# One level of Strassen for the first product of the MLP, in eight of nine token tiles

## The chip, the core and the metric

The kernel runs on one core of a Trainium2 chip. The core has a matrix engine (TensorE, "PE" in the profile, with its weight loads shown apart as "PEld"), a vector engine (VectorE, "DVE"), an activation engine (ScalarE, "ACT"), a general engine (GpSimd, "POOL") and a queue for transfers (SyncE, "SP"). [...] The metric is the device time of one execution, in microseconds (us).

## The reference

What is computed, cut to what matters:

```python
# q, k, v: [8 batches, 8 heads, 576, 64], s: [8, 8, 576]; attention with a bias of cumulated s
x = attention(q, k, v, s)                      # [8, 576, 512]
u = x + real(fft(fft(x, axis=1), axis=2))
un = (u - mean(u)) / sqrt(var(u) + 1e-6)       # over the 512 channels
out = u + maximum(un @ w_ch1, 0) @ w_ch2       # w_ch1 [512, 2048], w_ch2 [2048, 512]
```

The change is in the last line alone, the MLP, and mostly in its first product `un @ w_ch1`.

## The kernel before

The 8 x 576 = 4608 tokens run as eight batches through attention and the Fourier step, which write `u` to a buffer `uD` in DRAM (channels on partitions). Then the MLP runs over nine tiles of 512 tokens (`TOK`). Its data are held in two parts, a high part that the matrix engine takes in its short fp32 form (`F32R`) and a low part, the rest; each product is therefore three matmuls (high x high, low weights x high, high weights x low).

`mlp_tile(t0, n)` walks over 16 slices `f` of 128 hidden channels (`NF` = 16). For each it issues 12 matmuls of 128x512 (L182: three kinds times four blocks `j` of 128 channels) into one PSUM bank `h`, then the relu on ACT (`zh`, L186) and its low part on DVE (`zl`, L187), and, one slice later, 12 matmuls of 128x512 of the second product (L195 to L197) into four banks `acc0` to `acc3` that are held over the whole tile. The scale 1/std (`r`) is applied at the end of the tile, so that the first product runs on `u - mu`, split into `uch` and `ucl`.

`load_w(pool, f)` puts slice `f` of both weight matrices into SBUF for good: `wh[f]` and `wl[f]`, 1024 columns each, of which the first 512 belong to the first product and the rest to the second. The weights arrive as 64-bit numbers. `rounded` turns 256 columns of them into f32 with DVE (L82, L84, L86, L87), ACT (L83) and POOL (L88). For slices 0 to 5 (`NC` = 6) that was done earlier, during attention, and the f32 weights lie in a DRAM buffer `wD`; slices 6 to 15 are rounded while the first MLP tile runs. After that ACT casts the high part (L111) and DVE (first half) or POOL (second half) subtracts for the low part (L113).

`ln_tile` makes `uch`, `ucl`, `mu` and `r` of the next tile: it loads `u` (1 MB), sums over channels by matmuls with ones (L122), and uses DVE (L145, L147, L153, the reciprocal L158), ACT (L146, L148) and POOL. The first tile runs woven with the Fourier step of the last batch (lines L250 to L328, tiles `pzs`, `pzc`, `pyc`, `pys`) and with the rounding of the weights. The order on each engine is set by a scheduler from the order in which the generators are woven; nothing is written out by hand. At the end of a tile DVE multiplies `acc` by `r` (L203), POOL rebuilds `u` from `uch + ucl + mu` (L209, L210) and adds it (L211), and SP stores the result. In the last tile that sum is made ahead (L169) and added on DVE (L205).

## Time and profile before

| | us |
|---|---|
| timed runs, median (lowest to highest of 3) | 1440.1 (1437.15 to 1442.24) |
| profiled execution, its span | 1436.6 |
| attention, Fourier, up to the first MLP tile | 0 to about 587 |
| first MLP tile, woven with the last batch and the rounding of weights | 587 to 714.8 |
| tiles 1 to 8 | 714.8 to 1431.0 |
| last multiply, add and store | 1431.0 to 1436.6 |

One execution is profiled. "PE busy" counts overlapping pipelined matmuls, each of which is shown from issue to its modelled end, so the length of one row (about 0.39 us for 128x512) is not its cost in a stream: the distance from one start to the next is. Where the timeline folds several equal instructions into one row (x4), its start is that of the first. Tables by stage give, for each stretch of time, the busy time of each engine with the number of instructions in brackets, then the mean granted clock of the matrix engine (1.00 is full), the share of the transfer engines' time and GB/s.

### The profile page before, as it was taken

What the parts mean: (1) busy time and instruction counts of PE and PEld (TensorE: products, weight loads), DVE (VectorE), ACT (ScalarE), POOL (GpSimd) and SP (SyncE); (2) the same over time, 40 slices, a digit from 0 to 9 for tenths busy, and PEclk for the clock granted to TensorE, in tenths of its full rate; (3) what the DMA queues carried; (4) which work ended last, traced back from release to release, by engine and by line L of the source; (5) the groups of instructions that cost most, each with busy time, mean ns of one, the idle gap of its engine ahead of it and who ended that gap; (6) DMA issues with size and microseconds to landing.
All of it is one profiled execution on the core that took longest, in us unless ns stands there. A gap on an engine that the chain in (4) does not pass through costs nothing.

```text
span 1436.6 us, 17960 instructions
## 1 busy us (share of the span) xinstructions
PE 1333.6 (93%) x6190; PEld 1072.2 (75%) x6190; DVE 746.5 (52%) x1684; ACT 540.7 (38%) x1211; POOL 550.9 (38%) x540
## 2 busy tenths in 40 slices
PE   4888979898989897998899999999999999999998
...
DVE  6577676778676778799833232132321323212212
...
GB/s 208 128 185 146 152 145 168 148 159 181 156 144 164 163 121 162 173 122 119 93 23 30 30 30 8 22 30 30 30 8 22 30 30 30 8 22 0 30 0 30
DMA packets 78166, 124.98 MB, mean 87 GB/s; under 512 B 11256, under 2 KB 36185, under 8 KB 78075
## 3 DMA queue, kind: packets, MB, share of 16 engines
...
q8 instruction: 49, 0.80, 0.2%
...
## 4 chain that ended last, share of the span: by engine, by line
PE 50%; DVE 7%; POOL 2%; DMA 1%; issue 1%; ACT 1%; SPq 0%; DVEq 0%; POOLq 0%; ACTq 0%
PE h L182 25%; PE acc L195 8%; PE acc L197 8%; PE acc L196 8%; POOL we L88 1%; DVE we L82 1%; DVE wm L87 1%; DVE wl L113 1%; DVE wm L84 1%; DVE we L86 1%; DVE Df L259 0%; POOL wl L113 0%; DMA raw<-in_wP_dram 0%; ACT wh L111 0%; DVE ucl L147 0%
## 5 line engine op out<-in xcount | busy, mean ns | idle before, releaser
L187 DVE SCALAR_TENSOR_TENSOR zl<-h,zh 128x512 fp32r<-128x512 f32 x144 | 98.6, 686 | 402.1 <-ACT zh L186 402.1
L186 ACT ACTIVATE zh<-h 128x512 fp32r<-128x512 f32 x144 | 85.8, 596 | 524.8 <-PE h L182 524.8
L197 PE MATMUL acc<-zl,wh 128*128 128x512 f32 x576 | 226.6, 394 | 4.2 <-DVE zl L187 4.2
L195 PE MATMUL acc<-zh,wh 128*128 128x512 f32 x576 | 227.2, 394 | 0.4 <-ACT zh L186 0.4
L196 PE MATMUL acc<-zh,wl 128*128 128x512 f32 x576 | 226.3, 393 | 0.0
L520 PE MATMUL pavB<-P,va 128*128 128x320 f32 (+2 forms) x640 | 200.8, 403 | 7.4 <-ACT stage L524 6.7
L456 PE MATMUL pm<-KQ 128*128 128x256 f32 (+4 forms) x384 | 159.6, 434 | 38.7 <-DVE Mx L463 18.9
L492 ACT ACTIVATE P<-ps 128x320 f32<-128x320 f32 (+4 forms) x384 | 145.5, 391 | 114.8 <-PE ps L489 109.7
L488 PE MATMUL ps<-KQ 128*128 128x256 f32 (+3 forms) x384 | 155.0, 406 | 22.7 <-ACT P L492 15.8
L182 PE MATMUL h<-uch,wh 128*128 128x512 f32 x576 | 159.0, 396 | 8.3 <-ACT wh L111 8.3
L463 DVE CUSTOM_DVE_ANT_0 trash<-pm,amask 128x128 bf16<-128x128 f32 (+3 forms) x256 | 123.6, 483 | 76.4 <-PE pm L456 60.0
L182 PE MATMUL h<-uch,wl 128*128 128x512 f32 x576 | 159.0, 398 | 0.8 <-DVE wl L113 0.8
L182 PE MATMUL h<-ucl,wh 128*128 128x512 f32 x576 | 158.4, 396 | 0.0
L211 POOL TENSOR_TENSOR o<-o,w 128x512 f32<-128x512 f32 x32 | 42.1, 1316 | 249.6 <-issue 216.5
L182 PEld LDWEIGHTS h<-uch,wh 128*128 128x128 f32 x576 | 107.6, 189 | 35.7 <-ACT wh L111 12.0
L197 PEld LDWEIGHTS acc<-zl,wh 128*128 128x128 f32 x576 | 108.3, 188 | 30.8 <-DVE zl L187 5.8
L520 PEld LDWEIGHTS pavB<-P,va 128*128 128x128 f32 (+1 forms) x640 | 106.5, 197 | 31.1 <-issue 13.0
L182 PEld LDWEIGHTS h<-uch,wl 128*128 128x128 f32 x576 | 109.4, 190 | 26.7 <-DVE wl L113 1.5
L182 PEld LDWEIGHTS h<-ucl,wh 128*128 128x128 f32 x576 | 109.7, 190 | 25.0
L195 PEld LDWEIGHTS acc<-zh,wh 128*128 128x128 f32 x576 | 108.5, 188 | 25.3 <-ACT zh L186 0.8
L196 PEld LDWEIGHTS acc<-zh,wl 128*128 128x128 f32 x576 | 108.5, 188 | 24.8
L489 PE MATMUL ps<-q,k 128*128 128x256 f32 (+3 forms) x384 | 121.4, 319 | 0.0
(139 smaller groups left out, 2025.9 us busy)
## 6 DMA issues: line engine op xcount, KB each, us to landing
...
```

The lines of the kernel that those rows point to most:

```text
L182: nc.tensor.matmul(h[:, :n], a[:, j * 128:(j + 1) * 128], b[:, j, :n], start=i == 0, stop=i == 11)
L186: nc.scalar.activation(zh[:, :n], h[:, :n], AF.Relu)
L187: nc.vector.scalar_tensor_tensor(out=zl[:, :n], in0=h[:, :n], scalar=0.0, in1=zh[:, :n].bitcast(F32), op0=ALU.max, op1=ALU.subtract)
L195: nc.tensor.matmul(acc[j][:, :n], a[:, cs], y[:, :n], start=g == 0, stop=False)
L196: nc.tensor.matmul(acc[j][:, :n], b[:, cs], y[:, :n], start=False, stop=False)
L197: nc.tensor.matmul(acc[j][:, :n], a[:, cs], z[:, :n], start=False, stop=g == NF - 1)
L456: nc.tensor.matmul(p[:nq, :n], qy[:, h, 128 * c:128 * c + nq], ky[:, h, k0:k0 + n], start=True, stop=True)
L463: nc.vector.tensor_tensor_reduce(out=trash[:nq, :n], in0=p[:nq, :n], in1=amask[:nq, m0:m0 + n], scale=1.0, scalar=first if x else NEG, op0 ...
L488: nc.tensor.matmul(p[:nk, :n], ky[:, h, ksl], qy[:, h, a:a + n], start=True, stop=False)
L489: nc.tensor.matmul(p[:nk, :n], k1[:, h, ksl], q1[:, h, a:a + n], start=False, stop=True)
L492: nc.scalar.activation(P[:nk, o:o + a + n - lo], p[:nk, lo - a:n], AF.Exp, scale=0.125)
L520: nc.tensor.matmul(p[:, a - lo:n], va[:nk, c, vs], P[:nk, o:o + w], start=c == 0, stop=c == cs[-1])
```

## The change

The first product of tiles 1 to 8 is no longer computed slice by slice. Two hidden slices `f` = 2g and 2g+1 form a pair `g` (eight pairs). The 256 x 512 block of weights of the pair is seen as 2 x 2 blocks, and so is the tile's 512 channels x 512 tokens; one level of Strassen (Winograd's form) gives the four result blocks from seven products instead of eight. Each product is 6 matmuls of 128x256 (three kinds times two blocks of 128 channels; L338). Per pair there are 7 x 6 = 42 matmuls of 256 columns where there were 24 of 512. The four sums of weight blocks per pair are made once (`sums_w`: on POOL L144, DVE L153, L158, L161, L164, splits on ACT L148 and DVE L149) and kept in `sh[g]`, `sl[g]` (one sum overwrites `wh`, `wl`); the four sums of data blocks are made for each tile (`combine`, L230 to L233) and all seven blocks are split (`block`: ACT L221, DVE L222). The results are gathered out of PSUM by ACT copies (L342, L346, L348) and DVE adds (L344, L350, L353) before the relu (L330, L331).

The second halves of the weights no longer stay in SBUF. For slices 6 to 15 they are rounded as before and stored to `wD` (L120), and `load_w2(f)` loads 256 KB from there (L127), casts (ACT, L128) and subtracts (POOL, L129) for each slice of each of the nine tiles, into four buffers used in turn. `u` for the last addition is loaded again from `uD` rather than rebuilt (L275; in the last tile L268).

The first tile (`first_tile`) keeps the plain product, in two halves of 256 tokens (24 matmuls of 128x256 for each slice, L299). The second product is the same 12 matmuls of 128x512 (L249 to L251). In tiles 1 to 8 the order on the matrix engine is the order of the code: the pair before has 24 matmuls of the second product left, in 8 groups of 3, and after each of the seven block products stands one of these groups (after the last, two).

```diff
-            m = wl[:, xs].bitcast(F32) if f < NC else (yield from rounded(stage, f, x, nstage))
-            nc.scalar.copy(wh[:, xs], m)
...
-            (nc.vector if x * n < 512 else nc.gpsimd).tensor_sub(wl[:, xs], m, wh[:, xs].bitcast(F32))
...
-                for a, b in ((wh, uch), (wl, uch), (wh, ucl)):
-                    for j in range(4):
-                        nc.tensor.matmul(h[:, :n], a[:, j * 128:(j + 1) * 128], b[:, j, :n], start=i == 0, stop=i == 11)
...
+        wh = pool.tile([128, 512], F32R, tag=f"wh{f}", name=f"wh{f}")
+        wl = pool.tile([128, 512], F32R, tag=f"wl{f}", name=f"wl{f}")
         W[f] = (wh, wl)
         if f < NC:
+            nc.sync.dma_start(out=wl.bitcast(F32), in_=wD[f, :, 0:512])
+            nc.scalar.copy(wh, wl.bitcast(F32))
+            yield 0.2
+            nc.vector.tensor_sub(wl, wl.bitcast(F32), wh.bitcast(F32))
+            yield 0.2
+            return
+        for x in range(1024 // WC):
+            xs = slice(WC * x, WC * x + WC)
+            m = yield from rounded(stage, f, x, nstage)
+            if x < 2:
+                nc.scalar.copy(wh[:, xs], m)
+                yield 0.1
+                nc.vector.tensor_sub(wl[:, xs], m, wh[:, xs].bitcast(F32))
+            else:
+                nc.sync.dma_start(out=wD[f, :, xs], in_=m)
+            yield 0.1
...
+    def load_w2(f):
+        h = w2p.tile([128, 512], F32R, tag="w2h", name="w2h", bufs=4)
+        low = w2p.tile([128, 512], F32R, tag="w2l", name="w2l", bufs=4)
+        nc.sync.dma_start(out=low.bitcast(F32), in_=wD[f, :, 512:1024])
+        nc.scalar.copy(h, low.bitcast(F32))
+        nc.gpsimd.tensor_sub(low, low.bitcast(F32), h.bitcast(F32))
+        W2[f] = (h, low)
+    def sums_w(g):
+        (ah, al), (ch, cl) = W[2 * g], W[2 * g + 1]
+        sh = sp.tile([128, 768], F32R, tag=f"sh{g}", name=f"sh{g}")
+        sl = sp.tile([128, 768], F32R, tag=f"sl{g}", name=f"sl{g}")
+        def tmp():
+            return sx.tile([128, 256], F32, tag="sx", name="sx", bufs=5)
+        def whole(h, low, x):
+            t = tmp()
+            xs = slice(256 * x, 256 * x + 256)
+            nc.gpsimd.tensor_add(t, h[:, xs].bitcast(F32), low[:, xs].bitcast(F32))
+            return t
+        def parts(t, h, low):
+            nc.scalar.copy(h, t)
+            nc.vector.tensor_sub(low, t, h.bitcast(F32))
+        a21 = whole(ch, cl, 0)
+        a22 = whole(ch, cl, 1)
+        nc.vector.tensor_add(a22, a21, a22)
+        yield 1.0
+        parts(a22, ch[:, 0:256], cl[:, 0:256])
+        a11 = whole(ah, al, 0)
+        s2 = tmp()
+        nc.vector.tensor_sub(s2, a22, a11)
+        parts(s2, sh[:, 0:256], sl[:, 0:256])
+        yield 1.0
+        nc.vector.tensor_sub(a21, a11, a21)
+        parts(a21, sh[:, 256:512], sl[:, 256:512])
+        a12 = whole(ah, al, 1)
+        nc.vector.tensor_sub(a12, a12, s2)
+        parts(a12, sh[:, 512:768], sl[:, 512:768])
+        yield 1.0
+        SW[g] = (sh, sl)
...
+    def block(t0, k, src):
+        h = bp.tile([128, 2, 256], F32R, tag="bh", name="bh", bufs=9)
+        low = bp.tile([128, 2, 256], F32R, tag="bl", name="bl", bufs=9)
+        nc.scalar.copy(h, src)
+        nc.vector.tensor_sub(low, src, h.bitcast(F32))
+        BL.setdefault(t0, {})[k] = (h, low)
+    def combine(t0):
+        u, _ = LN[t0]
+        b11, b12, b21, b22 = (quarter(u, i, k) for i in range(2) for k in range(2))
+        t3, t2, t4 = (ltmp(x).rearrange("p (j t) -> p j t", j=2) for x in ("t3", "t2", "t4"))
+        nc.gpsimd.tensor_sub(t3, b22, b12)
+        nc.vector.tensor_sub(b12, b12, b11)
+        nc.vector.tensor_sub(t2, b22, b12)
+        nc.vector.tensor_sub(t4, b21, t2)
+        return [b11, b21, t2, b12, t3, b22, t4]
...
+        def issue(entry, j):
+            acc, y, z, f, done = entry
+            a, b = W2[f]
+            cs = slice(j * 128, (j + 1) * 128)
+            nc.tensor.matmul(acc[j], a[:, cs], y, start=f == 0, stop=False)
+            nc.tensor.matmul(acc[j], b[:, cs], y, start=False, stop=False)
+            nc.tensor.matmul(acc[j], a[:, cs], z, start=False, stop=f == NF - 1)
+            if f == NF - 1:
+                done(j)
...
+                w = op.tile([128, TOK], F32, tag="w", name="w", bufs=2)
+                nc.sync.dma_start(out=w, in_=uD[j, :, t0:t0 + TOK])
+            nc.vector.tensor_mul(o, r, acc[j])
+            (nc.vector if last else nc.gpsimd).tensor_add(o, o, w)
+            (nc.scalar if last and j % 2 else nc.sync).dma_start(out=out[j, :, t0:t0 + TOK], in_=o)
...
+            if f + 1 < NF:
+                load_w2(f + 1)
+            wh, wl = W[f]
+            h = bank("h")
+            for k in range(2):
+                i = 0
+                for a, b in ((wh, 0), (wl, 0), (wh, 1)):
+                    for j in range(4):
+                        nc.tensor.matmul(h[:, 256 * k:256 * k + 256], a[:, j * 128:(j + 1) * 128], bl[j // 2, k][b][:, j % 2], start=i == 0, stop=i == 11)
+                        i += 1
+            zh = zp.tile([128, TOK], F32R, tag="zh", name="zh", bufs=3)
+            zl = zp.tile([128, TOK], F32R, tag="zl", name="zl", bufs=3)
+            nc.scalar.activation(zh, h, AF.Relu)
+            nc.vector.scalar_tensor_tensor(out=zl, in0=h, scalar=0.0, in1=zh.bitcast(F32), op0=ALU.max, op1=ALU.subtract)
...
+    def fast_tile(t0, side):
+        _, r = LN[t0]
+        bl = BL.pop(t0)
+        acc = done = None
+        for g in range(NF // 2):
+            load_w2(2 * g)
+            load_w2(2 * g + 1)
+            todo = groups()
+            n = len(todo)
+            (ah, al), (ch, cl) = W[2 * g], W[2 * g + 1]
+            sh, sl = SW[g]
+            lo, hi = slice(0, 256), slice(256, 512)
+            A = [(ah[:, lo], al[:, lo]), (ah[:, hi], al[:, hi]), (sh[:, 0:256], sl[:, 0:256]), (ch[:, lo], cl[:, lo]),
+                 (sh[:, 256:512], sl[:, 256:512]), (sh[:, 512:768], sl[:, 512:768]), (ch[:, hi], cl[:, hi])]
+            b1 = hx.tile([128, 512], F32, tag="hx", name="b1") if g % 2 == 0 else bank("b1")
+            b2, b3 = bank("b2"), bank("b3")
+            cs = cp.tile([128, 3, 256], F32, tag="cs", name="cs", bufs=2)
+            z = [[zp.tile([128, TOK], F32R, tag=t, name=t, bufs=3) for t in ("zh", "zl")] for _ in range(2)]
+            def relu(y, at, src):
+                nc.scalar.activation(y[0][:, at], src, AF.Relu)
+                nc.vector.scalar_tensor_tensor(out=y[1][:, at], in0=src, scalar=0.0, in1=y[0][:, at].bitcast(F32), op0=ALU.max, op1=ALU.subtract)
+            for k, (p, start) in enumerate(((b1, True), (b2, True), (b1, False), (b3, True), (b1, False), (b3, False), (b1, False))):
+                bh, low = bl[k]
                 i = 0
+                for a, b in ((A[k][0], bh), (A[k][1], bh), (A[k][0], low)):
+                    for j in range(2):
+                        nc.tensor.matmul(p[:, 0:256], a[:, j * 128:(j + 1) * 128], b[:, j], start=start and i == 0, stop=i == 5, skip_group_check=not start)
                         i += 1
+                p = p[:, 0:256]
+                if k == 0:
+                    nc.scalar.copy(cs[:, 0], p)
+                elif k == 1:
+                    nc.vector.tensor_add(cs[:, 0], cs[:, 0], p)
+                elif k == 2:
+                    nc.scalar.copy(cs[:, 1], p)
+                elif k == 3:
+                    nc.scalar.copy(cs[:, 2], p)
+                elif k == 4:
+                    nc.vector.tensor_add(cs[:, 2], cs[:, 2], p)
+                    relu(z[1], hi, cs[:, 2])
+                elif k == 5:
+                    nc.vector.tensor_add(cs[:, 1], cs[:, 1], p)
+                    relu(z[0], slice(0, 512), cs[:, 0:2].rearrange("p a t -> p (a t)"))
+                else:
+                    relu(z[1], lo, p)
+                for x in range(n * k // 7, n * (k + 1) // 7):
+                    todo[x]()
+                side(g, k)
+            if g == 0:
+                acc = accs()
+                done = writer(t0, acc, r)
+            held.extend((acc, z[x][0], z[x][1], 2 * g + x, done) for x in range(2))
...
+    def early(t0):
+        blocks.extend(combine(t0))
+        for k in range(5):
+            block(t0, k, blocks[k])
+            yield 1.0
+    blocks = []
+    weave([first_tile(tiles[0]), NF], [chain(idle(1000), mixing), FOURIER * 0.6], [ahead(), 100],
+          [later(chain(ln_tile(tiles[1], 1), early(tiles[1])), 4), 16])
+    for _ in feed:
+        pass
+    for k in range(5, 7):
+        block(tiles[1], k, blocks[k])
+    for g in range(2):
+        weave([sums_w(g), 1.0])
...
+            if x == 1 and k % 2 == 0 and g + 2 < NF // 2:
+                if k == 0:
+                    adding[0] = sums_w(g + 2)
+                next(adding[0], None)
```

The matrix engine inside a tile, before: `h` is the bank of the first product, `acc` those of the second; after three rows of four L182, one for each kind, stand groups of three L195, L196, L197 (three of the four groups are shown).

```order
2998 L182 MATMUL h<-uch,wh_7463 128x512 x4
2999 L182 MATMUL h<-uch,wl_7464 128x512 x4
3000 L182 MATMUL h<-ucl,wh_7463 128x512 x4
3001 L195 MATMUL acc_8317<-zh,wh_7384 128x512 [waits Activation_49]
3002 L196 MATMUL acc_8317<-zh,wl_7385 128x512
3003 L197 MATMUL acc_8317<-zl,wh_7384 128x512 [waits DVE_49]
3004 L195 MATMUL acc_8318<-zh,wh_7384 128x512
3005 L196 MATMUL acc_8318<-zh,wl_7385 128x512
3006 L197 MATMUL acc_8318<-zl,wh_7384 128x512
3007 L195 MATMUL acc_8319<-zh,wh_7384 128x512
3008 L196 MATMUL acc_8319<-zh,wl_7385 128x512
```

The matrix engine in the first pairs of a later tile, after: `b` are the banks of the block products, `bh` and `bl` the split data blocks, `sh` and `sl` the split weight sums, `w2h` and `w2l` the second weights.

```order
2684 L338 MATMUL b_8344<-bh,sh_8088 128x256 [waits Activation_49]
2685 L338 MATMUL b_8344<-bh,sh_8088 128x256
2686 L338 MATMUL b_8344<-bh,sl_8089 128x256 x2
2687 L338 MATMUL b_8344<-bl,sh_8088 128x256 x2
2688 L249 MATMUL acc_8196<-zh,w2h 128x512
2689 L250 MATMUL acc_8196<-zh,w2l 128x512
2690 L251 MATMUL acc_8196<-zl,w2h 128x512
2691 L338 MATMUL b_8346<-bh,wh_6607 128x256 x2
2692 L338 MATMUL b_8346<-bh,wl_6608 128x256 x2
2693 L338 MATMUL b_8346<-bl,wh_6607 128x256 x2
2694 L249 MATMUL acc_8194<-zh,w2h 128x512
2695 L250 MATMUL acc_8194<-zh,w2l 128x512 [waits Pool_49]
```

Between block products of half width there now stands a group of three of the second product, and a product that adds to a bank which ACT has just copied waits for ACT.

The vector engine late in the first tile, before: only the rounding (L82 to L87), the low part of the weights (L113) and, now and then, `zl`.

```order
1339 L82 TENSOR_SCALAR we<-raw 128x256 [waits DMAHW1_49,Pool_49]
1340 L84 TENSOR_SCALAR wm<-raw 128x256
1341 L87 SCALAR_TENSOR_TENSOR wm<-raw,wm 128x256 [waits DVE_49]
1342 L86 SCALAR_TENSOR_TENSOR we<-raw,we 128x256 [waits Activation_49]
1343 L113 TENSOR_TENSOR wl_7385<-we,wh_7384 128x256 [waits Activation_49]
1344 L82 TENSOR_SCALAR we<-raw 128x256 [waits DMAHW2_49]
1345 L84 TENSOR_SCALAR wm<-raw 128x256
1346 L113 TENSOR_TENSOR wl_7385<-we,wh_7384 128x256 [waits Activation_49]
1347 L87 SCALAR_TENSOR_TENSOR wm<-raw,wm 128x256 [waits DVE_49]
```

The same stretch after: sums of weight blocks (L161, L164) and their splits (L149, `sl`) stand among the rounding.

```order
1356 L149 TENSOR_TENSOR sl_8089<-sx,sh_8088 128x256
1357 L304 SCALAR_TENSOR_TENSOR zl<-h,zh 128x512 [waits Activation_49]
1358 L118 TENSOR_TENSOR wl_7495<-we,wh_7494 128x256 [waits Activation_49]
1359 L82 TENSOR_SCALAR we<-raw 128x256 [waits DMAHW3_49,DMAHW2_49]
1360 L84 TENSOR_SCALAR wm<-raw 128x256
1361 L164 TENSOR_TENSOR sx<-sx 128x256
1362 L87 SCALAR_TENSOR_TENSOR wm<-raw,wm 128x256 [waits DVE_49]
1363 L86 SCALAR_TENSOR_TENSOR we<-raw,we 128x256 [waits Activation_49]
1364 L82 TENSOR_SCALAR we<-raw 128x256 [waits DMAHW4_49]
1365 L84 TENSOR_SCALAR wm<-raw 128x256
1366 L149 TENSOR_TENSOR sl_8089<-sx,sh_8088 128x256 [waits Activation_49]
```

Each of these rows pushes the rounding rows behind it back on the same engine.

The transfers at the start of the first tile, before, on SP: three loads of 512 KB of f32 weights behind the small transfer `rows`.

```order
490 L266 DMA rows<-xs 1x16x36 [waits DMAHW4_49,DMAHW3_49]
491 L106 DMA wl_6570<-wD 128x1024 [waits DMAHW5_49]
492 L106 DMA wl_6577<-wD 128x1024 [waits DMAHW6_49,PE_49]
493 L106 DMA wl_6613<-wD 128x1024 [waits DMAHW7_49,PE_49]
494 L77 DMA raw<-in_wP_dram 128x512 [waits DMAHW0_49]
```

And after: the second weights of slices 0 and 1 come first, behind `rows`, and the first weights in half the size.

```order
490 L417 DMA rows<-xs 1x16x36 [waits DMAHW4_49,DMAHW3_49]
491 L127 DMA w2l<-wD 128x512 [waits DMAHW5_49,PE_49]
492 L127 DMA w2l<-wD 128x512 [waits DMAHW6_49]
493 L106 DMA wl_6598<-wD 128x512 [waits DMAHW7_49]
494 L106 DMA wl_6603<-wD 128x512 [waits DMAHW0_49]
495 L106 DMA wl_6608<-wD 128x512 [waits DMAHW1_49]
496 L77 DMA raw<-in_wP_dram 128x512 [waits DMAHW2_49]
```

The load `w2l` of slice 0, which the second product of the first slice reads, now stands behind `rows<-xs`, which waits for the last fold of the Fourier step; before, those weights were in SBUF already.

210 lines of the change are left out of this document (107 added, 103 removed).

## The prediction

> **What bounds the kernel now.** I read the head of the page first (busy time by engine, the slices, the chain that ended last), then a table by stage, then the timeline inside one tile.
>
> ```profile
> span 1436.6 us, 17960 instructions
> PE 1333.6 (93%) x6190; PEld 1072.2 (75%) x6190; DVE 746.5 (52%) x1684; ACT 540.7 (38%) x1211; POOL 550.9 (38%) x540
> PE   4888979898989897998899999999999999999998
> DVE  6577676778676778799833232132321323212212
> ...
> core 0: us, PE busy (x) PEld busy (x) DVE busy (x) ACT busy (x) POOL busy (x), PEclk, DMA share, GB/s
> 587.00:640.00 53.00, 50.09 (x242) 40.86 (x241) 45.75 (x97) 20.92 (x48) 29.34 (x33) 0.96 0.40 136
> 640.00:699.00 59.00, 50.12 (x199) 36.97 (x197) 55.55 (x127) 27.60 (x63) 34.28 (x41) 0.97 0.39 131
> 699.00:715.00 16.00, 11.95 (x38) 8.74 (x37) 14.21 (x24) 7.60 (x16) 11.14 (x9) 0.79 0.05 9
> 715.00:1431.00 716.00, 715.75 (x3101) 581.68 (x3099) 208.93 (x269) 125.13 (x213) 154.08 (x116) 1.00 0.06 23
> ```
>
> In the slices (35.9 us each) DVE shows 9, 9, 8 in the 18th to 20th and falls to 3 in the 21st, from where PE stays at 9. From 715 to 1431 us PE is busy for 715.75 of 716 us at full clock while DVE uses 29%, ACT 17% and POOL 22%: tiles 1 to 8 are bound by PE and by nothing else. From 640 to 699 us it is the other way: DVE is busy 55.55 of 59 us (94%), PE 50.12, which is 85% although its overlapping rows hide gaps. The waits in the first tile say the same:
>
> ```profile
> PE h L182 <- ACT wh L111: 8.3, 7, 2.3
> PE acc L197 <- DVE zl L187: 4.2, 3, 2.4
> ```
>
> PE waits there for weights that DVE and POOL have rounded, and for DVE's `zl`. So the change touches two stretches with opposite limits: it takes work from PE where PE is the bound, and gives work to DVE where DVE is.
>
> **Tiles 1 to 8: the price of a matmul.** The stream has 716 us for 8 x (384 + 4) = 3104 matmuls of 512 columns: 0.2307 us each. One slice `f` shows the same:
>
> ```profile
> 1003.42 1.07 PE L182 MATMUL h<-uch,wh 128*128 128x512 f32 x4
> 1008.86 0.84 PE L182 MATMUL h<-uch,wh 128*128 128x512 f32 x3
> ```
>
> 5.44 us for 24 matmuls (0.227); the mean over all tiles is the 0.2307 that I use. The change does the first product of a tile in 8 x 42 = 336 matmuls of 256 columns where there were 192 of 512. In columns that is 7/8. What a 256-column matmul costs in a stream is the question, since each still loads 128 columns of weights. The Fourier step shows two streams of nearly that form:
>
> ```profile
> 623.28 0.87 PE L283 MATMUL pzs<-dsin,Do 128*96 128x256 f32 x6
> 623.99 0.87 PE L291 MATMUL pzc<-dcos,De 128*96 128x258 f32 x6
> 624.79 0.36 PE L293 MATMUL pzc<-cor,eh 33*96 33x258 f32 x1
> ...
> 630.02 1.38 PE L314 MATMUL pys<-ssin,zs 96*128 96x290 f32 x9
> 631.24 1.37 PE L305 MATMUL pyc<-scos,zc 97*128 97x290 f32 x9
> ...
> L283 PEld LDWEIGHTS pzs<-dsin,Do 128*96 128x96 f32 x18 | 2.7, 180 | 2.8 <-DVE Do L69 1.1 <-DVE zl L187 1.0 <-ACT Do L68 0.4
> L182 PEld LDWEIGHTS h<-uch,wh 128*128 128x128 f32 x576 | 107.6, 189 | 35.7 <-ACT wh L111 12.0
> ```
>
> Six of 256 columns take 0.71 us (0.118 each). Nine of 290 columns, with loads 128 columns wide as in the changed kernel, take 1.22 us (0.1356); 34 columns fewer at 0.2307/512 each give 0.120. I take 0.119. The low end is half of 0.2307, 0.115; the high end is the run of L291, 0.80/6 = 0.133, which ends on a short weight load of another shape. Per tile: 336 x 0.119 = 40.0 against 192 x 0.2307 = 44.3, so -4.3 us, and -34 us over eight tiles. At 0.115 it is -45, at 0.133 it is +3.
>
> [...]
>
> **What must keep up with PE there.** A pair `g` becomes 42 x 0.119 + 24 x 0.2307 = 10.5 us.
>
> ```profile
> L187 DVE SCALAR_TENSOR_TENSOR zl<-h,zh 128x512 fp32r<-128x512 f32 x144 | 98.6, 686 | 402.1 <-ACT zh L186 402.1
> L186 ACT ACTIVATE zh<-h 128x512 fp32r<-128x512 f32 x144 | 85.8, 596 | 524.8 <-PE h L182 524.8
> L68 ACT CAST zs<-pzs x24: 350/368/372, 146.9 to 628.1; 96x256 fp32r<-96x256 f32 x24
> L69 DVE TENSOR_TENSOR zs<-pzs,zs x24: 399/420/421, 147.3 to 628.6; 96x256 fp32r<-96x256 f32 x24
> L113 POOL TENSOR_TENSOR wl<-wl,wh 128x512 fp32r<-128x512 f32 x3 | 4.5, 1523 | 2.0 <-ACT wh L111 1.9
> ```
>
> DVE: three adds and two half-wide `zl` at 0.42 (a 256-column read of PSUM), one full at 0.69: 2.8 us. ACT: three copies and two relus at 0.37, one at 0.60, two casts of second weights at about 0.6: 3.6. POOL: two subtractions of 1.52: 3.0. Beside that, `combine` and `block` put six more operations of 512 columns on DVE in each tile than `ucl` did (three sums, and seven splits for four), some 4 us of 85, and three more casts on ACT; POOL loses the eight additions of L209 and L210. All stay below half of 10.5. The order on PE now has waits: a product that adds to a bank waits for the copy from it. Between the two products on one bank stand two groups of three (0.69 each) and a product (0.71), 2.1 us for a copy of 0.37 or an add of 0.42: no stall, priced 0. What is behind such a wait on PE is everything, so 0.25 us per pair would already cost 64 x 0.25 = 16 us; that is a rival. The loads of second weights are free of the path if they come within the turn of four buffers, about 5 us after the slot is given back. In the rows
>
> ```profile
> 595.74 0.50 SPq L266 DMA_DIRECT2D rows<-xs  x1
> 596.29 1.53 SPq L106 DMA_DIRECT2D wl<-wD  x3
> 600.99 1.14 ACT L111 CAST wh<-wl 128x512 fp32r<-128x512 f32 x2
> ```
>
> three loads of 512 KB in one queue give the first cast after 4.7 us; 256 KB alone should need about half. Eight tiles read 33.6 MB, 47 GB/s over 716 us, on top of 23 GB/s. Priced 0. On SP these loads can stand behind an output store that waits for POOL at the end of a tile; that delay is under the 5 us, too.
>
> **The first tile.** It has no block products, so no gain; 24 x 0.119 for 12 x 0.2307 is +0.09 us per slice, hidden while DVE is the bound. What it gets is the preparation. Counted in the order on DVE, from the second-last fold of the Fourier step to the last low part of the weights, these stand there in addition: 33 operations of `sums_w` on 256 columns, five splits of data blocks less one `ucl`, seven operations of 512 columns (LN and `combine` of tile 1), a reciprocal; and two rounding operations fewer. All of DVE in that stretch of before, and the reciprocal:
>
> ```profile
> L86 DVE SCALAR_TENSOR_TENSOR we<-raw,we 128x256 int32<-128x256 int32 x27 | 15.7, 583 | 0.4 <-ACT we L83 0.2
> L87 DVE SCALAR_TENSOR_TENSOR wm<-raw,wm 128x256 f32<-128x256 uint16 x25 | 13.5, 540 | 0.5
> L82 DVE TENSOR_SCALAR we<-raw 128x256 int32<-128x256 int32 x27 | 11.0, 415 | 0.0
> L84 DVE TENSOR_SCALAR wm<-raw 128x256 int32<-128x256 int32 x24 | 10.1, 419 | 0.0
> L113 DVE TENSOR_TENSOR wl<-we,wh 128x256 fp32r<-128x256 f32 x15 | 7.6, 511 | 1.9 <-ACT wh L111 1.8
> L187 DVE SCALAR_TENSOR_TENSOR zl<-h,zh 128x512 fp32r<-128x512 f32 x8 | 5.4, 680 | 0.4 <-ACT zh L186 0.4
> L145 DVE TENSOR_TENSOR u<-u,mu 128x512 f32<-128x512 f32 x1 | 0.9, 861 | 0.3 <-ACT mu L139 0.3
> ...
> L158 DVE RECIPROCAL r<-r 128x512 f32<-128x512 f32 x8 | 26.8, 3348 | 4.0 <-ACT r L157 4.0
> ```
>
> The seven rows add up to 64.2 us where DVE was busy 55.55, since neighbours overlap: one operation occupies 0.865 of its row. So 33 x 0.511 + 4 x 0.69 + 7 x 0.86 - 2 x 0.42 = 24.8, times 0.865 is 21.5, and 3.35 for the reciprocal: 24.8. DVE had 7 us idle from 587 to 640 and 3.5 after; the first few sums stand in the first of these stretches. I take 23 that last. Low end: all idle filled, 24.8 - 10.5 = 14. High end: the added operations at the slowest price that DVE shows for such a piece, 0.82 (below), unoverlapped: 33 x 0.82 + 9 + 3.35 = 39. ACT's casts (0.4) and POOL's sums of the same groups lie beside it: POOL loses its twenty 256-column subtractions here and gets 16 of 512 and about 16 sums, and was at 58%.
>
> Two smaller things. The second weights of slice 0 stand behind `rows` on SP, so its first group waits some 5 us (4.7 from load to cast as above, less for the smaller size, and 1.5 of POOL); PE has 59 - 50 = 9 to spare before 699, so 0, with 5 as the high end. And the turn to tile 1:
>
> ```profile
> 701.51 0.41 DVE L113 TENSOR_TENSOR wl<-we,wh 128x256 fp32r<-128x256 f32 x1
> 714.78 1.09 PE L182 MATMUL h<-uch,wh 128*128 128x512 f32 x4
> ```
>
> 12.9 us from the last low part to tile 1. Those 12.9 hold LN work that the new order does earlier, but the last slice's second weights now go DVE, POOL, store, load, ACT, POOL, behind six sums on POOL (0.87 each): I take +1.5, between -4 and +8.
>
> **Sum.** -34 + 23 + 1.5 = -9.5 on the profiled 1436.6: 1427. The median of the timed runs, 1440.1, is 3.5 above that span; the forecast is 1430.
>
> **Rivals.**
>
> Hidden sums (faster, further): DVE's extra work fills its idle time and that of the turn, so that the first tile loses 10 or less: 1440.1 - 34 + 10 = 1416 or below, down to 1406. For it: 10.5 us idle on DVE, and LN leaving the turn. Against it: 94% busy where the added rows stand. 0.16.
>
> Nothing (within 4.3 us): the first tile costs 30 to 39, or a matmul 0.126 (336 x 0.126 = 42.3, -16 in all) with the 23: 1436 to 1444. For it: the row of 0.133. 0.18.
>
> The other side, one mechanism: DVE slows beside a busier POOL. The same operation on the same data takes
>
> ```profile
> 699.83 0.82 DVE L82 TENSOR_SCALAR we<-raw 128x256 int32<-128x256 int32 x1
> 700.77 0.28 DVE L82 TENSOR_SCALAR we<-raw 128x256 int32<-128x256 int32 x1
> ```
>
> 0.82 beside a running POOL add and 0.28 without. If POOL's added second-weight subtractions put another 20 or so of the 100 rounding operations from 0.28 to 0.82 (+11 us) and hold the sums at 0.82 (39), the first tile loses 50: 1440 - 34 + 50 = 1456. It decides from a loss of 39 on. 0.10. [...]
>
> Waits on PE in the pairs: 0.25 us for each of 64 pairs, 1446; 0.5 us, 1462. Against it: 2.1 us of room for 0.4 of work. 0.07.
>
> Weight loads set the pace: every matmul of 256 columns waits for a load of 0.189. Then 336 x 0.189 = 63.5 per tile, +19.2 instead of -4.3: 1440 + 154 + 24 = 1618. Against it: the six of L283 came each 0.118 with loads shown as 0.180, so recorded loads overlap. 0.04. [...]
>
> **How the numbers follow.** The forecast's own case, a gain of 5 to 23 us, 0.45; with hidden sums 0.61 for faster by over 0.3% (4.3 us, about what a measurement of this kernel can tell from no change). Same 0.18. Slower 0.10 + 0.07 + 0.04 = 0.21. Its own range is 1417 to 1435. For 8 in 10 I go from 1408 (most of the hidden sums) to 1450 (all of the nothing, about half of contention and waits).
>
> **What the changed profile would show.** Right: in tiles 1 to 8 PE busy throughout, a pair every 10.5 us, a tile in 85.2 instead of 89.5; L338 starts 0.119 apart; tile 1 starting near 740 instead of 714.8; DVE over 94% busy from 640 to 725, with L149 to L164 near 0.5. Wrong: waits of L338 on ACT or DVE, or of L250 on POOL in tiles 1 to 8 (handoffs); L338 starts over 0.126 apart; a first tile that ends before 728 (sums hidden) or after 755 (contention).

## The result and the profile after

The changed kernel takes 1505.3 us (1501.6 to 1507.6) where the kernel before took 1440.9 in the same session: the ratio is 1.045, interval 1.0425 to 1.0473. The forecast was 1430 with a range of 1408 to 1450; the change is slower. The profiled execution has a span of 1504.4, 67.8 over the one before.

The head of the page, as before: span, busy time by engine, slices of PE, DVE and the clock.

```profile
span 1504.4 us, 22206 instructions
PE 1331.1 (88%) x7534; PEld 1126.7 (75%) x7534; DVE 916.7 (61%) x2034; ACT 717.4 (48%) x1641; POOL 690.6 (46%) x644
PE   4988979889898987777759999999999999999998
DVE  6677677677767676969894453545536354453423
PEclk9998989999899988898879999999999999999999
```

PE is as busy as before, in a longer span. The slices fall to 7 and 5 in the first MLP tile (17th to 21st), the clock with them. The table by stage, with the columns as before (the first two stretches go from the last fold of the Fourier step to the last low part of the weights):

```profile
601.00:675.00 74.00, 55.44 (x295) 45.65 (x296) 59.33 (x112) 28.87 (x64) 45.06 (x42) 0.88 0.31 104
675.00:752.00 77.00, 56.12 (x269) 47.29 (x268) 71.20 (x159) 30.83 (x67) 41.25 (x44) 0.83 0.48 146
752.00:775.00 23.00, 10.29 (x48) 8.33 (x48) 22.89 (x33) 9.58 (x23) 17.22 (x18) 0.67 0.39 125
864.00:1497.00 633.00, 614.46 (x3745) 544.17 (x3744) 287.53 (x482) 252.89 (x538) 229.72 (x170) 0.99 0.26 80
```

In tiles 2 to 8 PE is now idle for 18.5 of 633 us and the clock is 0.99; before, in tiles 1 to 8, these were 0.25 of 716 us and 1.00. What PE waits for, from the last fold on:

```profile
PE b L338 <- ACT cs L346: 19.8, 13, 3.1
PE acc L249 <- ACT w2h L128: 19.4, 2, 11.9
PE h L299 <- ACT wh L116: 18.7, 11, 4.1
PE b L338 <- DVE cs L350: 5.6, 3, 4.2
```

The first and the last row are handoffs in tiles 1 to 8, the second is a stop of 7.5 us at the first slice and one of 11.9 at the turn to tile 1, the third is the old wait for rounded weights.

The rate of the block products is the forecast's. From the timeline (starts of folded pairs of L338):

```profile
902.88 0.40 PE L338 MATMUL b<-bh,wh 128*128 128x256 f32 x2
903.12 0.40 PE L338 MATMUL b<-bh,wl 128*128 128x256 f32 x2
903.36 0.40 PE L338 MATMUL b<-bl,wh 128*128 128x256 f32 x2
903.59 0.40 PE L249 MATMUL acc<-zh,w2h 128*128 128x512 f32 x1
```

0.71 us for six, 0.118 each (forecast 0.119), and a pair without stops takes 10.53 (forecast 10.5). But tiles 2 to 7 take 90.2 us each (tile 6 takes 91.7) instead of 85.2. Tile 8, which has no next tile to prepare, does not lose this: its pairs take 10.53 to 10.56 us, but for one of 11.25. Where tile 2 loses most, in its third pair (14.7 us):

```profile
892.51 0.60 ACT L128 CAST w2h<-w2l 128x512 fp32r<-128x512 f32 x1
892.68 1.26 POOL L203 TENSOR_TENSOR t<-t,t 128x512 f32<-128x512 f32 x1 [0.74 <-ACT t L202]
...
893.97 0.62 ACT L68 CAST th<-t 128x512 fp32r<-128x512 f32 x1 [0.86 <-POOL t L203]
894.50 0.36 ACT L346 COPY cs<-b 128x256 f32<-128x256 f32 x1
...
894.91 0.50 PE L338 MATMUL b<-bh,sh 128*128 128x256 f32 x2 [2.38 <-ACT cs L346]
```

And stretches of 1 us after it, where the third number from the right is the granted clock:

```profile
896.00:897.00 1.00, 1.00 (x6) 0.91 (x5) 0.11 (x1) 0.00 (x0) 0.86 (x1) 0.73 0.00 0
897.00:898.00 1.00, 1.00 (x6) 1.00 (x5) 0.97 (x2) 0.00 (x0) 0.00 (x0) 0.50 0.39 121
898.00:899.00 1.00, 1.00 (x4) 0.64 (x4) 0.64 (x2) 0.33 (x1) 0.00 (x0) 0.50 0.38 141
899.00:900.00 1.00, 1.00 (x7) 1.00 (x6) 0.76 (x2) 0.18 (x2) 0.00 (x0) 0.56 0.06 16
900.00:901.00 1.00, 1.00 (x7) 0.85 (x6) 0.42 (x1) 1.00 (x3) 0.00 (x0) 1.00 0.00 0
```

The copy L346 takes 0.36 us, as priced. It stands in ACT's queue behind the cast of second weights and behind `th` of the next tile's LayerNorm, which waits for POOL; POOL had waited for ACT's squares. PE stops for 2.38 us, and from about 896.5 to 899.9 its granted clock is 0.50. The pair takes 14.73 us, which is 10.53 and the stop of 2.38 and 1.8 more, about half of these 3.4 us.

It was not always so. The same stop comes in the third pair of tiles 1 to 7 (2.34 to 2.38 us, 3.10 in tile 6). In tiles 1 and 4 the clock stays at 1.00 behind it, and the pair still takes 14.1 to 14.2 us, since a second handoff then comes too late. Tile 4:

```profile
1075.23 0.50 PE L338 MATMUL b<-bh,sh 128*128 128x256 f32 x2 [2.35 <-ACT cs L346]
...
1079.02 0.50 PE L338 MATMUL b<-bh,wh 128*128 128x256 f32 x2 [0.69 <-DVE cs L350]
```

DVE's add L350 stands there behind a sum of the next tile's data blocks (L232). In the tiles with the half clock, but for tile 6, the third pair takes 14.6 to 14.7, so the half clock itself adds only about 0.6 us to a tile.

Counted with the starts of the stages, the 67.8 us are:

| piece | forecast | measured |
|---|---|---|
| 8 x 336 narrow for 8 x 192 wide matmuls | -34 | -34 |
| stops and half clock in tiles 1 to 8: 10 in tile 1 (from 777.1 on), 31 in tiles 2 to 7, 1 in tile 8 | 0 | +42 |
| last fold to last low part: 105.7 (595.8 to 701.5) before, 150.5 (601.2 to 751.7) after | +23 | +45 |
| from there to tile 1: 13.3 before (701.5 to 714.8); 17.9 after (751.7 to 769.6, where the long stop ends), and 4.0 that the half clock and a wait for POOL cost up to 777.1 | +1.5 | +9 |
| start of the last fold: 595.8 before, 601.2 after (596.0 to 605.6 in the kernels below, but for the one that rounds more in attention) | 0 | +5 |
| from the last matmul to the end: 6.0 before, 7.4 after | 0 | +1 |

The pieces are rounded and add up to 68.

### The profile page after: what moved, and what is told of

Read it like the earlier page. It is cut to its first block, busy times and chain, and to the rows that moved or that the text cites. A ratio compares the mean times of both kernels' runs of the same rounds, so it can differ in the third digit from the quotient of the medians.

```text
span 1504.4 us, 22206 instructions
## 1 busy us (share of the span) xinstructions
PE 1331.1 (88%) x7534; PEld 1126.7 (75%) x7534; DVE 916.7 (61%) x2034; ACT 717.4 (48%) x1641; POOL 690.6 (46%) x644
## 4 chain that ended last, share of the span: by engine, by line
PE 35%; DVE 5%; DMA 4%; POOL 4%; ACT 2%; issue 2%; SPq 0%; POOLq 0%; ACTq 0%; DVEq 0%
PE b L338 17%; PE acc L249 6%; PE acc L250 6%; PE acc L251 6%; DMA u<-uD 2%; POOL t L203 2%; DMA w2l<-wD 2%; POOL w2l L129 1%; DVE t L191 1%; POOL t L189 1%; ACT w2h L128 1%; DVE sl L149 0%; DVE bl L222 0%; DVE we L86 0%; DVE wm L84 0%
## 5 line engine op out<-in xcount | busy, mean ns | idle before, releaser
L129 POOL TENSOR_TENSOR w2l<-w2l,w2h 128x512 fp32r<-128x512 f32 x144 | 190.1, 1321 | 385.1 <-ACT w2h L128 334.1
L249 PE MATMUL acc<-zh,w2h 128*128 128x512 f32 x576 | 232.6, 404 | 19.5 <-ACT w2h L128 19.4
L250 PE MATMUL acc<-zh,w2l 128*128 128x512 f32 x576 | 232.8, 404 | 3.0 <-POOL w2l L129 2.9
L251 PE MATMUL acc<-zl,w2h 128*128 128x512 f32 x576 | 230.8, 401 | 4.0 <-DVE zl L304 4.0
L639 PE MATMUL ps<-KQ 128*128 128x256 f32 (+3 forms) x384 | 152.7, 401 | 19.0 <-ACT P L643 12.2
L330 ACT ACTIVATE zh<-cs 128x256 fp32r<-128x256 f32 (+1 forms) x128 | 67.2, 525 | 162.0 <-DVE cs L350 98.6
L128 ACT CAST w2h<-w2l 128x512 fp32r<-128x512 f32 x144 | 88.8, 617 | 103.6 <-DMA w2l<-wD 103.1
L251 PEld LDWEIGHTS acc<-zl,w2h 128*128 128x128 f32 x576 | 110.9, 192 | 31.7 <-DVE zl L304 5.6
L249 PEld LDWEIGHTS acc<-zh,w2h 128*128 128x128 f32 x576 | 111.0, 193 | 26.7 <-ACT w2h L128 20.2
L350 DVE TENSOR_TENSOR cs<-cs,b 128x256 f32<-128x256 f32 x64 | 26.9, 420 | 159.7 <-PE b L338 159.6
L586 POOL TENSOR_TENSOR q<-qk,q 64x576 fp32r<-64x576 f32 x64 | 100.8, 1589 | 42.3 <-DMA q<-KQ 37.3
L338 PEld LDWEIGHTS b<-bh,wh 128*128 128x128 f32 x512 | 96.9, 190 | 29.8 <-DVE cs L350 7.2
L250 PEld LDWEIGHTS acc<-zh,w2l 128*128 128x128 f32 x576 | 111.0, 193 | 10.5 <-POOL w2l L129 5.4
L331 DVE SCALAR_TENSOR_TENSOR zl<-cs,zh 128x256 fp32r<-128x256 f32 (+1 forms) x128 | 72.5, 567 | 64.1 <-ACT zh L330 64.1
L338 PE MATMUL b<-bh,wh 128*128 128x256 f32 x512 | 102.9, 282 | 5.6 <-DVE cs L350 5.6
```

The costliest lines, as they stand in the source:

```text
L128: nc.scalar.copy(h, low.bitcast(F32))
L129: nc.gpsimd.tensor_sub(low, low.bitcast(F32), h.bitcast(F32))
L249: nc.tensor.matmul(acc[j], a[:, cs], y, start=f == 0, stop=False)
L250: nc.tensor.matmul(acc[j], b[:, cs], y, start=False, stop=False)
L251: nc.tensor.matmul(acc[j], a[:, cs], z, start=False, stop=f == NF - 1)
L338: nc.tensor.matmul(p[:, 0:256], a[:, j * 128:(j + 1) * 128], b[:, j], start=start and i == 0, stop=i == 5, skip_group_check=not start)
```

## Experiments on the first tile and the turn

All are the changed kernel with one edit, each timed in three rounds beside the kernel before; "stretch" is from the last fold (first `Aw` on DVE) to the last low part of rounded weights, 150.5 us in the changed kernel.

**Sums of weight blocks left out.** `sums_w` is not called, and the products take plain blocks.

```diff
-        ..., (sh[:, 0:256], sl[:, 0:256]), (ch[:, lo], cl[:, lo]), ...
+        ..., (ah[:, lo], al[:, lo]), (ch[:, lo], cl[:, lo]), ...
-        weave([sums_w(g), 1.0])
```

> The sums of weight blocks are left out (their places in the products are taken by plain blocks of the same size; the product itself is then not the MLP's), so that the matrix engine's work is the same. Theory B, the vector engine's occupancy sets the first tile: 33 operations at 0.44 us fewer before the last low part of the weights, so that comes 13 to 18 us earlier than 751.7, and with the turn to tile 1 the whole falls by 15 to 25, to 1480 to 1490. Rival: the first tile is late because the order on SP and PE delays the Fourier step (the rows of the last fold came 23 us later than before), and the sums fill gaps: the last low part comes less than 8 us earlier.

1475.3 us (1.023 of before, 1.0188 to 1.0278), 30 less, more than the 15 to 25 expected. The stretch is 134.0, 16.5 shorter, as theory B has it. The table by stage over the stretch, first of the changed kernel, then of this one:

```profile
601.00:752.00 151.00, 111.56 (x562) 92.94 (x562) 130.54 (x270) 59.70 (x130) 86.31 (x86) 0.85 0.40 125
```

```profile
602.00:736.00 134.00, 103.62 (x561) 87.41 (x562) 111.40 (x237) 53.99 (x113) 68.68 (x67) 0.90 0.45 141
```

DVE's busy time falls from 130.5 to 111.4 us for 33 operations, so that one of them cost 0.58, not 0.44 (this counts in whatever DVE's other operations gained without the part of the sums on POOL, which the run does not set apart). Another 13.6 come between the last low part and the start of tile 2 (112.6 us in the changed kernel, 99.0 here), at the turn and in tile 1, where the sums had stood on all three engines; PE's long stop at the turn falls from 11.9 to 2.9 us.

**First second-weights early.**

```diff
-        load_w2(0)
...
+    w2e = ctx.enter_context(pool("w2e"))
...
-          [chain(weights, *[load_w(w0, f) for f in range(N0)]), ...
+          [chain(weights, *[load_w(w0, f) for f in range(N0)], first_w2(0)), ...
```

> The second weights of slice 0 are loaded and split with the first weights of slices 0 to 2, before the last batch's folds, so that the second product of the first slice does not wait behind the transfer of rows (one temporary of the sums is dropped, 4 instead of 5, for its space). Theory C: the 7.5 us stop of PE at 599.6 and the half clock after it delay the Fourier step and with it all that follows: second products start near 596 instead of 607, the last low part 8 to 15 us earlier, the whole 8 to 15 us less, 1490 to 1497. Rival: DVE is the bound and has the delay absorbed: within 4 us of 1505.

1505.2 us (1.0437, 1.0397 to 1.0477): nothing. The second product starts at 598.8 instead of 607.1, the stretch is 149.1. Theory C falls; the 7.5 us stop is absorbed, as the prediction had it.

**Last half first.**

```diff
-        for x in range(1024 // WC):
+        for x in (2, 3, 0, 1) if f == NF - 1 else range(4):
```

> Of the last slice the second half of the weights is rounded, stored and loaded before the first half. Theory D: the turn from the last low part (751.7) to tile 1 is long since the second weights of slice 15 go DVE, POOL, store, load, ACT, POOL after everything else (a stop of 11.9 us): that stop falls under 5, the whole falls by 6 to 10, to 1495 to 1499. Rival: the chain of DVE operations of the first pairs is as late, and the stop only moves to the block products: within 3 us of 1505.

1503.1 us (1.0425, 1.0387 to 1.0463), within noise of 1505.3. The stop of 11.9 us is gone, but the last first-product slice starts 6 us later instead (755.2 against 748.9). Theory D in this form falls.

**LayerNorm of tile 1 later.**

```diff
-          [later(chain(ln_tile(tiles[1], 1), early(tiles[1])), 4), 16])
+          [later(chain(ln_tile(tiles[1], 1), early(tiles[1])), 9), 16])
```

> The LayerNorm, the block sums and splits of tile 1 are woven into the first tile five steps later (9 instead of 4), so that on DVE the rounding of slices 8 and 9 stands ahead of them again. Theory E: the first tile is late not only by DVE's added work (29 us busy) but since DVE waits in line (15 us more idle from the last folds to the last low part) behind LN operations that need PE, ACT and POOL while rounding that could run stands behind them. Then the first low part of slice 8 comes 10 or more earlier than 675, counted from the folds, and the whole falls by 8 to 16 us, to 1490 to 1497. Rival: the same DVE work is only moved later: the last low part does not move, within 4 us of 1505.

1508.3 us (1.0478, 1.044 to 1.0516): the first low part of slice 8 comes at 674.6 (675.1 in the changed kernel; counted from the folds 2.8 us earlier, where 10 were expected), and the stretch is 150.1. The work is only moved; theory E falls in this form.

**LayerNorm of tile 1 left out.**

```diff
-          [later(chain(ln_tile(tiles[1], 1), early(tiles[1])), 4), 16])
+          [later(chain(same(), early(tiles[1])), 4), 16])     # LN[tiles[1]] = LN[tiles[0]]
```

> Tile 1 gets the LayerNorm of tile 0 (its own, with the load of u, the sums, squares and the reciprocal on DVE, is left out; the block sums and splits stay), so tile 1's output is not the MLP of its own tokens. Priced by rows that is some 10 us of DVE in the first tile, about 5 of POOL, and the waits of DVE on POOL and ACT behind it. Theory E (DVE stands in line): 10 to 20 us earlier, 1485 to 1495. Rival: since the later place of the same LayerNorm brought nothing, only its DVE time counts: 4 to 9 us.

1494.3 us (1.0373, 1.0335 to 1.0412), 11 less, stretch 139.1: 11.4 shorter, of which 5.6 are DVE's busy time (124.9) and the rest idle time. That is within theory E's range, at its lower end.

**No second weights in the first tile** (from slice 2 on).

```diff
-            if f + 1 < NF:
-                load_w2(f + 1)
+            if f == 0:
+                load_w2(1)
+            elif f + 1 < NF:
+                W2[f + 1] = W2[(f + 1) % 2]
```

> In the first tile the second weights of slices 2 to 15 are neither loaded nor split; slices use those of 0 and 1 instead (the first 512 tokens then lack the true second product). Stores and tiles 1 to 8 stay. Theory F: POOL's 14 subtractions and the loads slow DVE's rounding, and the turn to tile 1 waits for slice 15: the last low part comes 5 to 10 us earlier, the stop of 11.9 us is gone, the whole falls by 12 to 20 us, to 1485 to 1493. Rival: the reload lies beside the bound: only the stop goes and the block products wait in its place, the whole falls by less than 5.

1490.4 us (1.0347, 1.0313 to 1.0381), 15 less; stretch 139.3, 11.2 shorter. Theory F holds: the stop of 11.9 is gone, too, though in tile 1 one of 5.9 for a copy on ACT comes up. I had priced POOL's 16 wide subtractions at nothing; with 14 of them left out, and their loads and casts, DVE's busy time falls from 130.5 to 122.9 us with the same 270 operations:

```profile
601.00:741.00 140.00, 108.91 (x569) 88.66 (x569) 122.91 (x270) 54.78 (x120) 73.39 (x76) 0.89 0.36 114
```

**All three left out.**

> Left out together: the sums of weight blocks, the first tile's second weights from slice 2 on, and the LayerNorm of tile 1 (places filled with other data of the same size, so the product is not the MLP's). If these three explain the first tile's loss of 45 us between the last folds and the last low part, that stretch falls from 150 back to 105 to 115 us, and the whole to 1455 to 1465. If the stretch stays above 125, something else in the change (the order itself, the stores of second halves, the splits) costs the rest.

1454.9 us (1.0094, 1.0056 to 1.0131), 50 less. The table by stage over its stretch:

```profile
598.00:714.00 116.00, 97.38 (x555) 79.58 (x556) 94.88 (x223) 42.72 (x91) 46.62 (x53) 0.96 0.43 138
```

116.0 us instead of 150.5, at the edge of what was expected: 34.5 of the 44.8 are these three (one by one 16.5, 11.2 and 11.4; they overlap by 5). DVE's busy time falls by about as much, from 130.5 to 94.9, which is 6 below the kernel before (100.9). The other 10 are not settled: DVE is idle for 21 us of the stretch here, and was for 5 before. PE's clock is back at 0.96.

**Sums all on DVE.**

```diff
-            nc.gpsimd.tensor_add(t, h[:, xs].bitcast(F32), low[:, xs].bitcast(F32))
+            nc.vector.tensor_add(t, h[:, xs].bitcast(F32), low[:, xs].bitcast(F32))
```

> The changed kernel with the four additions of each pair's weight sums on DVE instead of POOL: some 17 to 19 more operations on DVE in the first tile, 19 fewer on POOL. Theory of DVE's occupancy alone: 0.42 x 0.865 x 18 = 6.5 us more, 1508 to 1514. Theory G, beside a running POOL operation DVE's take longer (the 256-column sums took 0.71 in the mean where 0.41 is their undisturbed time): the other DVE operations get shorter by about as much as is added, the whole stays within 4 us of 1505 or falls.

1497.7 us (1.038, 1.0353 to 1.0407), 8 less, stretch 140.9. POOL's busy time from 595 us to the end of the stretch falls by 14 us (86.8 to 72.9), and DVE's does not rise (132.8 to 131.3), though it makes 39 operations of the sums where there were 33. Two prices in the timeline of the changed kernel:

```profile
609.15 0.42 DVE L149 TENSOR_TENSOR wl<-sx,wh 128x256 fp32r<-128x256 f32 x1
609.48 1.65 DVE L158 TENSOR_TENSOR sx<-sx 128x256 f32<-128x256 f32 x1
...
609.37 1.49 POOL L403 TENSOR_TENSOR Bw<-xa,xs 128x576 f32<-128x576 f32 x1 [0.94 <-DMA raw<-in_wP_dram]
```

The group of the splits in the stretch, in the changed kernel:

```profile
L149 DVE TENSOR_TENSOR sl<-sx,sh 128x256 fp32r<-128x256 f32 x12 | 9.1, 771 | 0.0
```

and in this one:

```profile
L149 DVE TENSOR_TENSOR sl<-sx,sh 128x256 fp32r<-128x256 f32 x9 | 4.6, 532 | 0.0
```

Two operations of one size, 0.42 and 1.65: the long one stands beside a POOL operation of 1.49. The timeline of the whole stretch says the same of the 33 operations of the sums on DVE: the ten that ran with POOL at rest took 0.41 us each, and the fifteen that took 0.93 or more all had POOL at work for 0.7 of their time or longer; the other eight took 0.41 or 0.42 with POOL at work for 0.46 of their time up to all of it. With fewer on POOL the mean of the splits falls from 0.771 to 0.532. That is theory G, though the number of sums before the last low part changed as well (25 and the 14 additions, where there were 33), so its share is not exact.

**More weights in attention**, on the hand order in its second form (below).

```diff
-NC = 6
+NC = 8
-NC1 = 4.5
+NC1 = 6.5
```

> As the order by hand in its second form, and the weights of slices 6 and 7 are rounded during attention, too (8 of 16 slices there instead of 6). If DVE's rounding in the first tile sets its end, 16 pieces fewer at 1.9 us each take up to 30 us from it, and attention, where DVE is busy 65 to 78%, takes back a part: 10 to 25 us less than with 6 slices. Rival: the Fourier step of the last batch and the place that it frees set the start of the later slices: within 5 us, or slower by what attention loses.

1538.4 us (1.0678, 1.063 to 1.0726), 35 more than the second form: the last fold comes at 648.8 instead of 600.1, while the stretch falls by 13.5. Attention has no room for them at this pace.

## Experiments on the stops in tiles 1 to 8

**Squares on DVE.**

```diff
-        nc.scalar.activation(t, u[:, 0], AF.Square)
+        nc.vector.tensor_mul(t, u[:, 0], u[:, 0])
...
-            nc.scalar.activation(t2, u[:, j], AF.Square)
-            nc.gpsimd.tensor_add(t, t, t2)
+            nc.vector.tensor_mul(t2, u[:, j], u[:, j])
+            nc.vector.tensor_add(t, t, t2)
```

> The squares of the next tile's LayerNorm and their sum go from ACT and POOL, which hand them to each other three times, to DVE; nothing else changes. Theory A: in tiles 1 to 8 PE stops because ACT's copy L346 stands behind squares and a cast that wait for POOL (2.4 us at the third pair), and each stop is followed by some 3.4 us at half clock. Then the third pair falls from 14.7 us to under 11.5, a tile from 90.2 to 86 to 87, and the whole by 25 to 35 us, to 1470 to 1480. Rival: the second weights (loads, casts) set the stops: the third pair stays above 13.5 and the whole within 8 us of 1505.

1488.5 us (1.0347, 1.0291 to 1.0403), 17 less, where 25 to 35 were expected. The third pair falls from 14.7 to between 11.1 and 11.5, but the fourth rises from 10.55 to 12.2 with a new wait, for DVE:

```profile
PE acc L251 <- DVE zl L331: 8.3, 6, 1.4
PE b L338 <- DVE cs L350: 2.9, 6, 0.6
PE b L338 <- ACT cs L346: 2.5, 8, 0.6
```

A tile takes 88.5; tile 2 starts 10 us earlier, of which 5 are an earlier last fold. The stop belongs to what stands ahead of the copy, and follows it to another queue.

**Order by hand on all engines.** `manual_schedule` gets ACT, DVE, POOL and SP beside PE; `ln_steps` and `sums_steps` cut the work beside the products into pieces.

```diff
-    order.enter_context(tc.manual_schedule(engines={mybir.EngineType.PE}))
+    order.enter_context(tc.manual_schedule(engines={ET.PE, ET.Activation, ET.DVE, ET.Pool, ET.SP}))
...
+                if k in (3, 5):
+                    w2_split(2 * g + (k - 3) // 2)
...
+            if (g, k) == (0, 2) or 1 <= g <= 4 and k in (1, 3, 6):
+                next(norm, None)
```

> In tiles 1 to 8 the order on ACT, DVE, POOL and SP is that of the code, too, as it was for PE alone; the next tile's LayerNorm is cut into thirteen short steps set between the block products, the split of second weights into the middle of a pair, and the sums of pairs 2 to 7 stay in tile 1 (in the changed kernel the scheduler had drawn those of pairs 2 and 3 into the first tile). Theory A: all stops in tiles 1 to 8 come from work of the next tile that stands in line ahead of the copies: tiles take 85 to 86.5 us instead of 90.2, and the first tile loses half the sums, 8 us; the whole is 1455 to 1470. Rival: a stop remains at the handoffs whatever the order, 0.3 or more for each pair: tiles above 88, the whole above 1475.

1544.4 us (1.073, 1.0691 to 1.077), worse by 39. Most pairs run at 10.5 to 11.5, but the second takes 16.5 to 18.4 and the sixth 14.1 to 15.0:

```profile
PE b L435 <- DVE cs L447: 42.9, 12, 5.2
```

My order had made two queues of its own: in the second pair ACT's cast of second weights waited for a load that stood on SP behind output stores, in the sixth DVE ran a reciprocal of 3.35 us, and then its sums waited 4.1 us for POOL, whose subtraction of second weights had waited for ACT's cast.

**The same with the later LayerNorm of tile 1.**

> The order by hand in tiles 1 to 8 and the later LayerNorm of tile 1 together. If both theories hold the gains add: 1440 to 1460, near the kernel before. If the later LayerNorm moves nothing, it is within 4 us of the order by hand alone.

1552.9 us (1.078, 1.0748 to 1.0812): 8 more than the order by hand alone, so no gain from it here either.

**Second form.** Loads of second weights ahead of the output stores, the reciprocal in four parts, the sums of data blocks one by one.

```diff
-                    w2_split(2 * g + (k - 3) // 2)
+                    w2_split(2 * g + (k - 4) // 2)
+            flush()                                # output stores, after the pair's w2_dma
...
+        for x in range(4):
+            nc.vector.reciprocal(r[:, 128 * x:128 * x + 128], r[:, 128 * x:128 * x + 128])
+            yield
```

> The order by hand again (sums of pairs 2 to 7 in tile 1, every engine in the order of the code), with the two places mended at which it stopped PE in each tile (6 to 8 us in the second pair, 4 in the sixth): the second weights of a pair are loaded ahead of the last output stores and cast later, and the reciprocal (3.35 us in one piece on DVE) and the sums of data blocks are cut into short steps. Theory A: a product after a copy waits only when the copy's engine stands in line behind something else; then all pairs take 10.5 to 11.0, a tile 85.2 to 86.5, and the whole is 1455 to 1470. Rival: other stops come up in their place: tiles above 88.

1503.1 us (1.0441, 1.0389 to 1.0493): still a tile of 90.3 in the mean, the rival's number, but with a single stop, in the second pair. Its timeline:

```profile
958.76 2.55 POOL L393 TENSOR_TENSOR o<-o,w 128x512 f32<-128x512 f32 x2 [1.26 <-DVE o L392]
964.08 1.26 POOL L393 TENSOR_TENSOR o<-o,w 128x512 f32<-128x512 f32 x1 [2.77 <-PE b L460]
965.30 1.71 POOL L132 TENSOR_TENSOR w2l<-w2l,w2h 128x512 fp32r<-128x512 f32 x1
967.06 0.49 PE L355 MATMUL acc<-zh,w2l 128*128 128x512 f32 x1 [3.05 <-POOL w2l L132]
```

The subtraction of second weights stands on POOL behind the output additions.

**Third form.** The split goes ahead of the second-product groups of its step.

```diff
+                if k in (4, 5):
+                    w2_split(2 * g + k - 4)
                 for x in range(n * k // 7, n * (k + 1) // 7):
                     todo[x]()
-                if k in (4, 6):
-                    w2_split(2 * g + (k - 4) // 2)
```

> The order by hand in its second form left one stop in each tile: in the second pair a second-product matmul waits 2.5 to 3.7 us for POOL's subtraction of second weights, which stands behind two output additions that wait for their loads. Here the split of second weights comes ahead of these (after the fifth and sixth product). Theory A: then no stop is left, all pairs take 10.5 to 11.0, a tile 85.0 to 86.0, and the whole falls by 30 to 40 us against the second form, to 1463 to 1473. Rival: each mended stop uncovers another: tiles above 88, the whole above 1485.

1472.3 us (1.020, 1.0173 to 1.0227), 31 less than the second form. Tiles 2 to 7 take 85.7 to 86.0, and from 860 us on the list of PE's waits is empty. The table by stage:

```profile
860.00:1460.00 600.00, 599.95 (x3724) 534.79 (x3722) 295.82 (x504) 243.19 (x541) 218.35 (x165) 1.00 0.27 85
```

Theory A is shown: all stops of tiles 2 to 8 were a matter of the other engines' order. What is left of the loss lies in the first tile, the turn, and tile 1, where sums stand between the products (its pairs take 11 to 20).

**No reload in the first tile.**

```diff
                 nc.sync.dma_start(out=wD[f, :, xs], in_=m)
+                nc.scalar.copy(W2[f][0][:, ys], m)
+                nc.gpsimd.tensor_sub(W2[f][1][:, ys], m, W2[f][0][:, ys].bitcast(F32))
...
-            if f + 1 < NF:
+            if f + 1 < NC:
                 load_w2(f + 1)
```

> As the third form, and in the first tile the second weights of slices 6 to 15 are split straight from the rounded piece (they are still stored for the later tiles) and not loaded again from DRAM. If the way through DRAM makes the turn to tile 1 long, 5 to 12 us less than the third form; if POOL's queue does, within 4 us of it.

1462.8 us (1.0162, 1.0123 to 1.0201), the best of those that still compute the whole MLP, and still slower than before. In the profiles tile 2 starts 6.5 us earlier, counted from the last fold, and the intervals of the two ratios overlap: a gain of some us, in favour of the way through DRAM as a part of the turn, and no more exact than that.

## Why the prediction was wrong

**Tiles 1 to 8: the rate was right, "no stall, priced 0" was not.** This is the step that failed first. The price of a product (0.118) and the pair (10.53) were right, and the hand order, which removes every stop, gives 85.7 a tile against the forecast's 85.2. But I compared the time between two products on a bank (2.1 us) with the length of the copy (0.37) and the load of each engine over a pair (below half). Neither says when the copy starts. It starts behind all that stands ahead of it on ACT (in tile 2 at 894.50, behind a cast begun at 893.97), and the scheduler, which orders every engine but PE, had put the next tile's LayerNorm there, a chain ACT, POOL, ACT. That is the rival "waits on PE in the pairs", to which I gave 0.07; its price came to 0.65 us per pair in tiles 2 to 7 (31.4 us over 48 pairs), of which the half clock is a small part (about 0.6 us in each tile that has it). Tile 8 of the changed kernel, without a next tile's work, shows the same as the hand order does. No row of before shows such a queue; the order did show it, and I had read it on PE and DVE alone.

**The first tile: the mechanism was right, the term too small.** +23 became +45. DVE's busy time rose by 29.6 (100.9 to 130.5 us): the sums cost 0.58 each instead of 0.44, beside a busier POOL. That part is the rival "DVE slows beside a busier POOL" in a milder form. The rows of 0.42 and 1.65 above agree with it. The other 15 are new idle time of DVE (5.1 us of 106 before, by the row below, 20.5 of 151 after): I let the added work fill idle time, and the idle time grew. I put that down to a queue with more operations that wait for others, but no run shows it: with the sums, the second weights and the LayerNorm all left out DVE is still idle for 21 us of 116. The longest waits on record are for `zl`, 10.6 us from 595 to 752, where the kernel before has 1.5 from 590 to 702. That ACT's and POOL's added work would lie beside it was wrong, for the second weights by 11 us. DVE's waits in the changed kernel from 595 to 752, the longest row, and the kernel before over its stretch:

```profile
DVE zl L304 <- ACT zh L303: 10.6, 4, 5.5
```

```profile
596.00:702.00 106.00, 92.53 (x401) 71.13 (x401) 100.90 (x226) 49.65 (x113) 61.15 (x69) 0.96 0.38 126
```

**The first second-weights behind `rows`: right** at 0, shown by their early load.

**The turn: +1.5 became +9,** outside the -4 to +8 by a little. The way through DRAM is not all of it: at the turn the load of slice 15 is issued at 760.9, but its cast on ACT stands behind a cast of tile 2's LayerNorm (the trace does not show when the load landed):

```profile
760.94 1.27 SPq L127 DMA_DIRECT2D w2l<-wD  x3
...
768.10 0.62 ACT L68 CAST th<-t 128x512 fp32r<-128x512 f32 x1 [3.21 <-DVE t L191]
768.62 0.40 ACT L148 CAST sh<-sx 128x256 fp32r<-128x256 f32 x1
768.93 0.61 ACT L128 CAST w2h<-w2l 128x512 fp32r<-128x512 f32 x1
769.59 0.80 PE L249 MATMUL acc<-zh,w2h 128*128 128x512 f32 x1 [11.88 <-ACT w2h L128]
```

That fits with the last half first, which brought nothing. From the last low part to the start of tile 2 it takes 112.6 us in the changed kernel, 106.2 without the reload of second weights and 99.0 without the sums of weight blocks. So the sums count for more there than the reload (the +1.5 had six of them on POOL in it); by how much the place of the cast counts was not taken apart.

**Weight loads: right that they do not set the pace.** All loads of a tile rise by 37% (388 to 532). In the hand order they are busy for 534.8 of 600 us and PE waits for none of them.

**Not counted:** the end after the last matmul, which is 1.4 us longer.

**Still open:** the new idle time of DVE in the first tile, and with it about 10 us of the stretch that remain with all three suspects gone; the start of the last fold, which moves by up to 10 us between kernels that are alike until there.
